# A hand-ordered step list for retention and a SoLU feed-forward block: zero products moved, steps re-ordered

## The chip, the cores and the metric

The kernel runs on one core of a Trainium2 chip. Its engines work from queues of their own and meet at semaphores: TensorE (PE: matrix products, with weight loads shown as PEld), VectorE (DVE), ScalarE (ACT), GpSimd (POOL) and SyncE (SP), which issues nearly all DMAs. The metric is the device time of one execution in microseconds; lower is better. The kernel before took 213.36 us as the median of three runs (212.89 to 214.8).

## The reference, cut to what matters

```python
# q, k, v: (8, 8, 576, 64) = batch, head, position, head_dim, float32
scores = q @ k.transpose(0, 1, 3, 2) / 8
D[h, i, j] = gamma[h] ** (i - j) if i >= j else 0      # gamma[h] = 1 - 2 ** (-5 - h)
x = (scores * D) @ v           # back to 4608 tokens x 512
h = x @ w_in                   # 512 -> 1024
e = exp(h - max(h));  sm = e / (sum(e) + 1e-9)
solu = h * sm
ln = (solu - mean(solu)) / sqrt(var(solu) + 1e-6) * g_ln
out = ln @ w_out               # 1024 -> 512, float32
```

First comes a retention (attention without softmax, with a decay by distance), then a feed-forward block with a softmax-weighted activation, a normalisation and a second product, for each of 4608 tokens.

## The kernel before, in words

**Tiles.** The tokens are cut into 18 tiles n = 0 to 17, each of 256 tokens in two halves i = 0, 1. Tiles 0 to 3 are the first 256 positions of four batch entries, 4 to 7 the next 256 of the same, 8 the last 64 of all four together; 9 to 17 repeat this for the other four entries. The retention is worked in chunks of 128 positions: products within a chunk, and a state that is carried from chunk to chunk.

**Steps.** The work on a tile is a set of small functions, each called a step. A word such as `mk:3.0.1` in the string ORDER (L744) calls step mk for tile 3, half 0, part 1; `@v`, `@s`, `@g` put it on VectorE, ScalarE or GpSimd. The words are run through once, each emits its instructions at that place in the queue of its engine, and nothing re-orders them later. So ORDER alone sets the order on every engine and on SyncE's DMA queue. A wait is added only where data or a buffer is needed, and it holds everything behind it on that engine.

For tile n the steps are:

- `lq`, `lk`, `lv` (L173): loads of 512 KB each from SyncE's queue, into 16 buffers that are used in turn; `wi`, `wo` load four chunks each of the two weights.
- `q`, `k`, `v` (L197, L152): casts to 16 bits, with the decay multiplied in where needed.
- `tp` (L239): 32 transposes of q and k on TensorE, copied out by two `qkT` steps (L150, L152); for some tiles a DMA transpose `dt` (L251) does both.
- `sc` (L265): 16 products q k within a chunk, for each half; `mk` (L276): four multiplications with the triangular mask, on VectorE.
- `kp` (L290): 32 products k v for the state; `t` (L305), `s32` (L314), `s16`: the state is added up, decayed and cast. `s32` is always on GpSimd.
- `xs` (L349): product with the carried state; `xv` (L364): 32 products of masked scores with v. Both write the same PSUM bank. `xT` copies the result out.
- `mm1` (L426): eight products with w_in (for tile 0's half 0 in four pieces of two, by chunk of w_in; `cwA` and `cwB` cast a chunk); `max` (L434), `exp` (L449), `solu` (L497), `nmu`, `sq` (L517), `w1`, `w2`, `pow`: softmax weight and normalisation.
- `lpj` (L584): 32 transposes, copied out by two `uTj` steps, or DMA transposes `du` (L591); `uc` subtracts the mean for the first tiles. `mm2` (L607): eight products with w_out, `osb` scales, `st` stores.
- `g32`, `ws`, `mean`, `mc`, `cw`: w_out is multiplied with g_ln and its mean taken off, early in the kernel. `gx` makes a decay table on ScalarE.

**Zero products.** `warm:k` (L720 to L729) issues k products of a tile of zeros, 128x128 by 128x512. They write the bank that the next step to take a bank will take, and that step overwrites them:

```python
junk = psum[:, int(BANKS[turns.get("bank", -1) + 1])]
zeros = s16s[:, 2 + 6 - 1].rearrange("p a e d -> p (a e d)")
for _ in range(k):
    nc.tensor.matmul(out=junk, lhsT=zeros[:, 0:P], rhs=zeros, start=True, stop=True)
```

There are 50 of them before, in eight groups: 21 before tp:0, 6 before sc:0.0, 4 before tp:1, 7 before tp:2, 2 before sc:2.1, 4 before kp:3, 4 before lpj:1 and 2 before lpj:2.

**Banks.** The string BANKS names, in the order in which steps ask for one, which of the eight PSUM banks a step gets.

The line numbers of the profile are those of the code below; in the changed kernel all lines behind ORDER stand one further down.

## Time and profile before

| | |
|---|---|
| median of 3 runs | 213.36 us (212.89 to 214.8) |
| the profiled execution, its time | 214.05 us |
| its span, first to last instruction | 212.3 us |
| TensorE busy, matmuls | 196.4 us (93%), 3154 |
| VectorE, ScalarE, GpSimd busy | 186.1, 171.0, 143.6 us |
| mean granted TensorE clock | 0.983 |
| products of `mm1` (L426) and `mm2` (L607) | 280 x 390 ns, 248 x 372 ns |
| zero products (L726) | 50, 379 ns each from start to end |
| bytes moved by DMA | 49.29 MB, mean 232 GB/s |

A profile page shows one execution. Busy shares are averages over the whole span; the stages have to be read apart, by slices or windows. Matmuls are pipelined: the time from the start to the end of one (379 ns) is longer than the time from one start to the next (216 ns at full clock), and the second is what a row of them costs. "Granted clock" is the share of full speed at which TensorE was allowed to run. A note such as `[0.54 <-ACT w_in L150]` behind an instruction says that its engine was idle for 0.54 us before it and that this ended when ScalarE's instruction of L150 was done; "issue" says that nothing which the profile shows was waited for.

### The profile page before, as it was taken

The page shows a single profiled execution, that of the slowest core. Times are in us where ns is not written, and L with a number is a line of the kernel's source. Part 1 is how long each engine was busy: PE and PEld are TensorE (multiplying, and loading weights), DVE is VectorE, ACT ScalarE, POOL GpSimd, SP SyncE. Part 2 cuts the span into 40 slices and gives each one's busy share as a digit, 9 for nine tenths or more (in the row PEclk, how much of TensorE's full clock was granted, in tenths as well). Part 3 has the DMA queues.
Part 4 walks back from the last instruction along what each step waited for, and adds up shares of the span by engine and source line. Part 5 has one row for each costly group of instructions (what it writes and reads, how often), then busy time and mean ns, then how long its engine had stood idle before and what let it go on. Part 6 is the DMA issues. An engine that isn't in the chain of part 4 may idle for free.

```text
span 212.3 us, 7613 instructions
## 1 busy us (share of the span) xinstructions
PE 196.4 (93%) x3154; PEld 103.2 (49%) x3154; DVE 186.1 (88%) x335; ACT 171.0 (81%) x288; POOL 143.6 (68%) x223
## 2 busy tenths in 40 slices
PE   4978979989998998999989999999999999999991
...
DVE  3499699999998999898979999999998999798960
...
PEclk9996799999999999999999999999999999999999
...
GB/s 162 290 383 310 281 296 367 295 259 262 138 217 183 213 209 216 320 293 223 249 327 164 285 236 316 279 197 246 264 203 217 238 99 179 171 148 115 85 198 150
DMA packets 90530, 49.29 MB, mean 232 GB/s; under 512 B 29440, under 2 KB 84992, under 8 KB 90496
## 3 DMA queue, kind: packets, MB, share of 16 engines
...
## 4 chain that ended last, share of the span: by engine, by line
PE 70%; DVE 14%; DMA 4%; SPq 4%; issue 3%; ACT 2%; POOL 1%; ACTq 0%; DVEq 0%; POOLq 0%
PE psum L426 25%; PE psum L607 24%; PE psum L265 5%; DVE nm L434 4%; PE psum L364 4%; DMA ld<-in_moe_w_in_dram 4%; PE psum L349 3%; PE psum L584 3%; SPq L173 3%; DVE u L497 2%; PE psum L290 2%; PE psum L239 1%; SPq L647 1%; PE psum L726 1%; DVE uc L553 1%
## 5 line engine op out<-in xcount | busy, mean ns | idle before, releaser
L426 PE MATMUL psum<-w_in,xT 128*128 128x512 f16 x280 | 68.5, 390 | 1.6 <-issue 0.7
L607 PE MATMUL psum<-w_out,uTj 128*128 128x512 f16 (+1 forms) x248 | 55.1, 372 | 0.0
L434 DVE TENSOR_REDUCE nm<-psum 128x1 f32<-128x1024 f32 x35 | 42.5, 1218 | 6.5 <-PE psum L426 6.1
L449 ACT ACTIVATE e<-psum,nm 128x1024 f32<-128x1024 f32 x35 | 39.0, 1114 | 11.0 <-DVE nm L434 9.2
L607 PEld LDWEIGHTS <-uTj 128*128 128x128 f16 x296 | 28.0, 98 | 31.0 <-issue 0.6
L497 DVE SCALAR_TENSOR_TENSOR u<-psum,e 128x1024 f16<-128x1024 f32 x35 | 42.0, 1216 | 0.4 <-ACT e L449 0.3
L517 ACT ACTIVATE sq<-u,nmu 128x1024 f16<-128x1024 f16 x35 | 40.3, 1150 | 1.2 <-DVE nmu L507 0.9
L426 PEld LDWEIGHTS <-xT 128*128 128x128 f16 x280 | 25.8, 100 | 31.3 <-issue 4.7
L540 POOL TENSOR_TENSOR rs<-w,mhalf 128x2 f32<-128x2 f32 x17 | 11.8, 696 | 38.0 <-DVE w L528 36.7
L197 POOL TENSOR_TENSOR v<-ld,small 128x512 f16<-128x512 f32 x29 | 30.4, 1057 | 4.6 <-DMA ld<-in_v_dram 3.5
L197 POOL TENSOR_TENSOR qk<-ld,small 128x512 f16<-128x512 f32 x24 | 25.0, 1050 | 1.1 <-DMA ld<-in_q_dram 0.6
L150 ACT COPY uTj<-psum 128x1024 f16<-128x1024 f16 (+1 forms) x18 | 17.3, 990 | 3.1 <-PE psum L584 3.1
L314 POOL TENSOR_TENSOR s32a<-t,small 128x256 f32<-128x256 f32 x16 | 10.6, 662 | 11.8 <-DVE t L152 6.9
L726 PE MATMUL psum<-s16s 128*128 128x512 f16 x50 | 14.2, 429 | 3.5 <-DVE s16s L853 3.1
L152 POOL CAST qk<-ld 128x512 f16<-128x512 f32 x25 | 15.4, 628 | 0.7 <-DMA ld<-in_k_dram 0.6
L150 ACT COPY qkT<-psum 128x1024 f16<-128x1024 f16 x12 | 12.0, 1018 | 4.7 <-PE psum L239 4.7
L265 PE MATMUL psum<-qkT 64*64 64x128 f16 x576 | 14.7, 223 | 0.2
L150 ACT CAST xT<-psum 128x512 f16<-128x512 f32 x24 | 13.3, 588 | 1.7 <-PE psum L349 1.0
L265 PEld LDWEIGHTS <-qkT 64*64 64x64 f16 x576 | 9.8, 107 | 7.5 <-issue 6.3
L364 PEld LDWEIGHTS <-v 64*64 64x64 f16 x576 | 9.3, 106 | 7.1 <-issue 6.8
L349 PE MATMUL psum<-qkT,s16s 128*128 128x128 f16 (+1 forms) x128 | 10.7, 216 | 1.6 <-POOL s16s L152 1.4
L314 POOL TENSOR_TENSOR s32b<-t,small 128x256 f32<-128x256 f32 x16 | 10.2, 640 | 2.0 <-DVE t L305 1.8
...
## 6 DMA issues: line engine op xcount, KB each, us to landing
...
```

What stands on the lines that cost most here:

```text
L150: nc.scalar.copy(out=out, in_=in_)
L197: vec(eng).tensor_tensor(out=to, in0=src, in1=tab[:, 8 * e : 8 * e + 8].unsqueeze(2).to_broadcast([P, H, D]), op=ALU.mult,)
L265: nc.tensor.matmul(out=s[o][cc, hp], lhsT=qkT_view(n, 1, c)[dd, e, hp], rhs=qkT_view(n, 0, c)[dd, :, hp], start=True, stop=True,)
L314: nc.gpsimd.tensor_tensor(out=s, in0=T["t", n, i], in1=gs.unsqueeze(2).to_broadcast([P, 4, D]), op=ALU.mult)
L349: nc.tensor.matmul(out=to, lhsT=state[:, hp].rearrange("p e d -> p (e d)"), rhs=rhs, start=first and hp == 0 and j == 0, stop=True, skip_g ...
L364: nc.tensor.matmul(out=x[c][oo, hp], lhsT=v16[cc, e, 2 * hp + o], rhs=T["ret", n, e, o][cc, hp], start=first[c] and e == 0 and hp == 0, st ...
L426: nc.tensor.matmul(out=h[:, a], lhsT=s[:, d], rhs=w_in16[:, d, a * 512 : (a + 1) * 512], start=r == 1, stop=r == 4,)
L434: nc.vector.tensor_reduce(out=nm, in_=T[key("h", n, i, j)], axis=AX.X if j is not None else AX.XY, op=ALU.max, negate=True)
L449: nc.scalar.activation(out=flat(e, j), in_=T[key("h", n, i, j)], func=ACT.Exp, bias=T["nm", n, i], accum_out=s)
L497: nc.vector.scalar_tensor_tensor(out=flat(u, j), in0=T[key("h", n, i, j)], scalar=1.0, in1=flat(T[key("e", n, i, j)], j), op0=ALU.mult, op ...
L517: nc.scalar.activation(out=t, in_=T[key("u", n, i, j)], func=ACT.Square, bias=T["nmu", n, i], accum_out=ss)
L607: nc.tensor.matmul(out=o, lhsT=T["uT", n, i][:, c], rhs=wt[:, c, a : a + w], start=c == 0, stop=c == NF - 1,)
```

## The change

Only the strings ORDER and BANKS differ. Every step of the computation is still there once, and no step's code is changed. There are 54 zero products instead of 50, in twelve groups: 17 before tp:0, 2 before sc:0.1, 3 before sc:0.0, 7 before tp:1, 2 before xv:0, 1 before sc:1.1, 10 before tp:2, 4 before xs:1.1, 2 before xv:1, 2 before kp:3, 1 before mm2:0.0 and 3 before xs:4.0. Some now stand ahead of `xs` and `xv`, where these are the first to write their bank. The other words are in a new order, most of all up to tile 9, and 67 steps run on another engine: among them 9 casts `k` go from GpSimd to ScalarE and 5 the other way, 4 casts `v` from VectorE to GpSimd, 4 `xT` from ScalarE to VectorE. From about tile 10 on the order is nearly the same. BANKS is a new assignment for the first two thirds.

The diff replaces all of ORDER; here are its beginning, two places in the middle and its end:

```diff
     ORDER = """
-        lk:0 gx lq:0 k:0.0@s k:0.1@g q:0.0@v lv:0 lq:1 q:0.1@v warm:21 tp:0 v:0.1@v v:0.0@v kp:0
-        q:1.1@v t:0.0@v s32:0.0 qkT:0.1@v qkT:0.0@s lk:1 k:1.0@v q:1.0@g warm:6 sc:0.0 t:0.1 wi:2
-        k:1.1@s sc:0.1 wi:0 wi:3 s32:0.1 mk:0.1.0 warm:4 tp:1 mk:0.0.0 mk:0.0.1 cwB:2@s s16:0.0@s
-        mk:0.1.1 xv:0 cwA:2@g wi:1 qkT:1.1@v cwA:0@v cwB:0@g xT:0.0@v cwB:3@g qkT:1.0@s sc:1.0
-        mk:1.0.1 xs:0.1 cwA:3@s mm1:0.0.3 lv:1 cwA:1@g xT:0.1@v s16:0.1@g cwB:1@s v:1.1@g mk:1.0.0
-        sc:1.1 mm1:0.0.0 lq:2 lk:2 q:2.1@g q:2.0@g mk:1.1.0 mm1:0.1 v:1.0@v mk:1.1.1 k:2.0@g
-        max:0.1 exp:0.1 mm1:0.0.2 mm1:0.0.1 max:0.0 k:2.1@v kp:1 t:1.0@s warm:7 tp:2 s32:1.0 lv:2
-        solu:0.1 v:2.1@v exp:0.0 s16:1.0@g qkT:2.1@s qkT:2.0@s t:1.1 v:2.0@g nmu:0.1 solu:0.0
-        xs:1.1 lq:4 xv:1 lv:3 lq:3 lk:3 xT:1.0@s nmu:0.0 warm:2 sc:2.1 sc:2.0 mk:2.1.0 xT:1.1@s
-        kp:2 q:4.1@g q:4.0@g s32:1.1 mk:2.0.0 t:2.0@s mk:2.1.1 mk:2.0.1 uc:0.1@s sq:0.1 mm1:1.1
-        s32:2.0 uc:0.0@v sq:0.0 max:1.1 xv:2 mm1:1.0 q:3.0@v xT:2.0@s exp:1.1 s16:2.0@g t:2.1
-        xs:2.1 max:1.0 xT:2.1@s solu:1.1 mm1:2.0 lpj:0 q:3.1@g max:2.0 wo:2 wo:0 v:3.0@g g32
-        k:3.1@g exp:1.0 mm1:2.1 solu:1.0 ws:4@s k:3.0@s wo:1 exp:2.0 w1:0@g v:3.1@g ws:0@g wo:3
-        ws:1@g ws:5@g ws:2@s w2:0 uTj:0.1@v uTj:0.0@v ws:3@s max:2.1 lk:4 w1:1@v nmu:1.1 nmu:1.0
-        ws:6@s warm:4 kp:3 ws:7@g t:3.0@s tp:3 solu:2.0 uc:1.0@v mm2:0.0 s32:3.0 qkT:3.0@s exp:2.1
-        s32:2.1 qkT:3.1@s lv:4 pow:0 t:3.1 k:4.1@s sq:1.0 mean k:4.0@g sc:3.1 sc:3.0 solu:2.1
-        nmu:2.0 mm2:0.1 v:4.1@v mc@s mk:3.1.0 mk:3.1.1 s16:3.0@g v:4.0@g lk:5 lk:6 mk:3.0.1
-        mk:3.0.0 sq:1.1 uc:1.1@s tp:4 s32:3.1 kp:4 lq:5 qkT:4.0@s cw:5@g xv:3 qkT:4.1@s osb:0.1@v
-        xs:3.1 t:4.0 warm:4 lpj:1 xT:3.1@s lq:6 cw:6@v sc:4.0 k:6.1@g nmu:2.1 xT:3.0@v s32:4.0
-        k:5.1@g lv:5 uTj:1.1@s s16:1.1@s cw:0@v uTj:1.0@s osb:0.0@s t:4.1 mk:4.0.0 uc:2.0@v mm1:3.0
-        w2:1 k:5.0@g q:5.1@g mm1:3.1 q:5.0@g pow:1 v:5.0@g s16:4.0@g max:3.0 uc:2.1@v s32:4.1 lk:7
-        sc:4.1 q:6.0@s q:6.1@s mk:4.0.1 v:5.1@g mm2:1.0 exp:3.0 max:3.1 st:0.1 lv:6 mk:4.1.0
-        mk:4.1.1 mm2:1.1 xv:4 w1:2@g xs:4.1 v:6.0@g solu:3.0 k:6.0@s v:6.1@g osb:1.0@s exp:3.1
-        solu:3.1 dt:5 kp:5 t:5.0 osb:1.1@s xs:4.0 tp:6 st:1.0 s16:2.1@g cw:1@v st:0.0 sq:2.0 kp:6
-        xT:4.1@s t:6.0 warm:2 lpj:2 s32:5.0 qkT:6.1@v t:5.1 xT:4.0@s qkT:6.0@s uTj:2.1@s cw:4@g
...
-        t:7.0 osb:3.1@s mm1:5.1 mk:7.0.0 sq:5.0 qkT:8.0@v nmu:4.0 sq:4.1 qkT:8.1@s sq:4.0 sc:7.1
-        mk:7.0.1 lv:9 s32:7.0 mm1:6.0 max:5.1 exp:5.1 s16:7.0@g mk:7.1.1 mk:7.1.0 max:6.0 lk:9
-        st:2.0 exp:6.0 st:2.1 s16:4.1@g q:9.1@g s16:3.1@g mm2:4.0 xs:7.0 s32:6.1 t:7.1 w2:4 pow:4
...
-        qkT:10.0@s qkT:10.1@v uTj:6.0@s mk:9.1.0 mk:9.1.1 w1:6@g sc:9.0 kp:10 mm1:8.0 max:7.1
-        mk:9.0.0 w2:6 t:10.0@s mk:9.0.1 lq:13 lk:12 s16:9.0@s q:11.0@g k:11.0@g s32:10.0 v:11.1@g
-        max:8.0 s32:9.1 xs:9.1 v:11.0@g exp:7.1 t:10.1 mm2:6.1 pow:6 st:5.0 s16:10.0@g w1:7@g
...
-        osb:15.1@v w2:17.0 w2:16 pow:16 w1:17.1 uT:17.1.0@s st:15.1 sq:17.1.1 sq:17.1.0 osb:16.1@v
-        pow:17.0 mm2:17.1.1 osb:17.0@s ssadd:17.1 w2:17.1 osb:16.0@v st:16.1 st:16.0 st:17.0
-        pow:17.1 osb:17.1.1@s mm2:17.1.0 st:17.1.1 osb:17.1.0@s st:17.1.0
+        lk:0 lq:0 k:0.0@v lv:0 lq:1 q:0.1@v q:0.0@v k:0.1@g warm:17 tp:0 v:0.1@v qkT:0.1@s
+        qkT:0.0@v v:0.0@g kp:0 gx warm:2 sc:0.1 warm:3 sc:0.0 lk:1 t:0.0@v mk:0.1.0 wi:0 q:1.1@g
+        q:1.0@g s32:0.0 mk:0.1.1 k:1.0@g mk:0.0.1 k:1.1@s s16:0.0@s warm:7 tp:1 xs:0.1 t:0.1
+        mk:0.0.0 cwA:0@v qkT:1.1@v cwB:0@s warm:2 xv:0 qkT:1.0@s wi:3 wi:2 warm:1 sc:1.1 s32:0.1
+        cwB:3@g xT:0.0@v mk:1.1.0 cwB:2@v sc:1.0 wi:1 cwA:3@s lv:1 cwA:2@g lq:2 xT:0.1@s mm1:0.0.3
+        mm1:0.0.0 cwA:1@v mk:1.1.1 mk:1.0.1 v:1.1@g mk:1.0.0 q:2.1@g lk:2 cwB:1@s k:2.0@g mm1:0.1
+        v:1.0@v max:0.1 exp:0.1 k:2.1@g lv:2 mm1:0.0.1 mm1:0.0.2 max:0.0 kp:1 t:1.0@s lq:3 s32:1.0
+        s16:1.0@g lk:3 exp:0.0 q:2.0@v solu:0.1 warm:10 tp:2 qkT:2.0@s warm:4 xs:1.1 nmu:0.1
+        qkT:2.1@s t:1.1 solu:0.0 v:2.1@v nmu:0.0 warm:2 xv:1 v:2.0@g sc:2.1 xT:1.1@s q:3.1@g kp:2
+        mk:2.1.1 sc:2.0 mk:2.1.0 w1:0@v lq:4 q:3.0@v mm1:1.1 sq:0.1 mk:2.0.1 mk:2.0.0 xT:1.0@s
+        t:2.0@s max:1.1 uc:0.0@v lv:3 uc:0.1@s s16:0.1@g s32:1.1 k:3.0@g k:3.1@g s32:2.0 s16:2.0@s
+        sq:0.0 mm1:1.0 t:2.1 w2:0 wo:0 xv:2 xs:2.1 max:1.0 xT:2.0@s mm1:2.0 exp:1.1 wo:3 xT:2.1@s
+        solu:1.1 exp:1.0 lpj:0 max:2.0 mm1:2.1 q:4.0@g g32 v:3.0@g v:3.1@g wo:1 uTj:0.1@v uTj:0.0@v
+        warm:2 kp:3 wo:2 ws:6@s solu:1.0 max:2.1 s32:2.1 tp:3 ws:0@g ws:7@g w1:1@g ws:1@g ws:3@s
+        exp:2.0 ws:4@s ws:2@s ws:5@g nmu:1.0 t:3.0@s solu:2.0 mean q:4.1@g lk:4 lq:5 uc:1.0@v
+        nmu:1.1 s32:3.0 lv:4 qkT:3.0@s warm:1 mm2:0.0 exp:2.1 mc@s qkT:3.1@s s16:3.0@g pow:0 t:3.1
+        k:4.0@g lk:5 k:4.1@s sc:3.1 solu:2.1 osb:0.0@s lv:6 sc:3.0 uc:1.1@s q:5.1@g tp:4 v:4.1@g
+        v:4.0@g mm2:0.1 cw:6@v mk:3.1.1 mk:3.0.1 mk:3.1.0 kp:4 k:5.1@g cw:5@g qkT:4.1@s mk:3.0.0
+        osb:0.1@v xv:3 v:6.1@g qkT:4.0@s t:4.0 sc:4.0 lpj:1 s32:4.0 xT:3.0@v s32:3.1 xs:3.1
+        mk:4.0.0 mk:4.0.1 sq:1.0 k:5.0@s lq:6 q:5.0@v xT:3.1@s mm1:3.0 lv:5 mm1:3.1 v:5.0@g v:6.0@g
+        max:3.0 sq:1.1 uTj:1.1@s lk:6 v:5.1@g k:6.1@g w1:2@g s16:4.0@g nmu:2.1 cw:0@v uTj:1.0@s
+        sc:4.1 t:4.1 max:3.1 q:6.0@s mk:4.1.0 nmu:2.0 mk:4.1.1 w2:1 exp:3.0 exp:3.1 k:6.0@s
+        warm:3 xs:4.0 q:6.1@s solu:3.0 solu:3.1 cw:1@v mm2:1.0 xv:4 xs:4.1 mm2:1.1 st:0.1 xT:4.0@s
+        xT:4.1@s kp:6 st:0.0 kp:5 uc:2.0@s uc:2.1@v t:6.0 s32:4.1 pow:1 cw:2@g tp:6 dt:5 osb:1.1@s
+        t:5.0 osb:1.0@s lpj:2 lk:7 lq:8 qkT:6.1@v lq:7 cw:7@v sc:5.0 s32:6.0 qkT:6.0@s t:6.1
+        mk:5.0.0 mm1:4.0 sq:2.0 uTj:2.0@s mm1:4.1 cw:3@v s32:5.0 cw:4@g q:7.0@g uTj:2.1@s sq:2.1
...
+        mk:7.0.1 osb:3.0@s st:2.1 w1:4@v qkT:8.1@v t:7.0 mk:7.0.0 mm1:5.1 sq:4.1 sc:7.1 qkT:8.0@s
+        mm1:6.0 s16:3.1@g v:8.1@g s32:7.0 q:9.0@g v:8.0@g q:9.1@g s32:5.1 w2:4 max:5.1 st:2.0
+        mk:7.1.0 k:10.0@s osb:3.1@s k:10.1@s s16:4.1@s mk:7.1.1 lk:9 exp:5.1 mm2:4.0 xs:7.0 lv:9
...
+        sc:9.0 kp:10 nmu:7.0 t:10.0@s sq:6.0 t:9.1 max:7.1 mk:9.0.0 mk:9.0.1 mm1:8.0 w2:6 s32:9.1
+        s16:9.0@g st:4.1 s32:10.0 max:8.0 mm2:6.1 t:10.1 s16:10.0@g exp:7.1 sq:7.0 solu:7.1
...
+        w2:17.0 w2:16 pow:16 w1:17.1 uT:17.1.0@v st:15.1 sq:17.1.0 osb:16.1@s sq:17.1.1 pow:17.0
+        mm2:17.1.1 osb:17.0@s ssadd:17.1 w2:17.1 osb:16.0@v st:16.1 st:16.0 st:17.0 pow:17.1
+        osb:17.1.1@s mm2:17.1.0 st:17.1.1 osb:17.1.0@s st:17.1.0
     """
...
     BANKS = "".join(
         """
-        765432765174630175237654736452316754230154673245345210765421076540156732473214065327640126
-        743025143761275463764521067531235076432016523767510643254016574237654103256743201765365721
-        034756201675436721045673210547623765401675473256107347652017654320176542365410756320174356
+        765476325176435201675432576432104567312310450176076354217645310725601327432765310247501675
+        435243150761276305674321045730176354210673201325764216574017654237654106523756401765362751
+        034726501675436721045673210547623765401765463257106347652017654320176542365410756320174356
         742340165746523765437653276
```

117 lines of the change are left out of this document (59 added, 58 removed).

## The prediction

> **What bounds the kernel now.** I read the page's 40 slices first. TensorE is at 9 tenths almost everywhere from slice 18 on and thinner before, and the granted clock has its one dip in slices 3 to 5:
>
> ```profile
> PE   4978979989998998999989999999999999999991
> DVE  3499699999998999898979999999998999798960
> PEclk9996799999999999999999999999999999999999
> ```
>
> The windows of 10 us (columns: stretch, length, busy us of PE, PEld, DVE, ACT, POOL, clock, DMA share, GB/s) give the stages.
>
> ```profile
> 20.00:30.00 10.00, 8.64 (x121) 3.82 (x117) 8.17 (x13) 4.16 (x7) 6.71 (x10) 0.78 1.11 284
> 40.00:50.00 10.00, 9.02 (x138) 4.38 (x138) 10.00 (x19) 9.31 (x16) 9.55 (x13) 1.00 1.04 271
> 70.00:80.00 10.00, 9.77 (x167) 5.57 (x167) 10.00 (x18) 8.69 (x15) 9.32 (x13) 1.00 1.16 224
> 140.00:150.00 10.00, 10.00 (x173) 5.46 (x170) 9.84 (x21) 9.94 (x16) 6.22 (x10) 1.00 0.95 243
> ```
>
> Up to 30 us nothing is full but the DMA; from 30 to 80 VectorE is, at 10.00 of 10 in three windows; from 120 to 200 TensorE has 10.00 in every window. TensorE's real products are the same in both kernels, so the time moves with what TensorE loses before about 112 us: idling, zero products (50, 0.216 us each at full clock) and half clock. I looked for these losses in TensorE's own waits and its timeline (start, us, what).
>
> ```profile
> 17.49 0.58 PE L349 MATMUL psum<-qkT,s16s 128*128 128x128 f16 x4
> 18.61 1.01 PE L426 MATMUL psum<-w_in,xT 128*128 128x512 f16 x2 [0.54 <-ACT w_in L150]
> 19.55 0.64 PE L265 MATMUL psum<-qkT 64*64 64x128 f16 x16
> 20.12 5.29 PE L426 MATMUL psum<-w_in,xT 128*128 128x512 f16 x14
> 25.34 0.45 PE L290 MATMUL psum<-v,qk 64*64 64x64 f16 x32
> 25.72 1.68 PE L726 MATMUL psum<-s16s 128*128 128x512 f16 x7
> 27.33 0.64 PE L239 MATMUL psum<-ident,qk 64*128 64x64 f16 x32
> 29.34 0.40 PE L349 MATMUL psum<-qkT,s16s 128*128 128x128 f16 x4 [1.36 <-POOL s16s L152]
> ```
>
> Fourteen mm1 products take 5.29 us: the clock is 0.5 from 17.75 to 24.39 us, each takes 0.427 instead of 0.216. The third loss has no partner:
>
> ```profile
> 66.90 0.45 PE L584 MATMUL psum<-ident,uc 64*128 64x64 f16 x19 [0.90 <-issue]
> 81.46 0.21 PE L364 MATMUL psum<-ret__1809,v 64*64 64x128 f16 x1 [0.73 <-issue]
> 110.64 0.82 PE L426 MATMUL psum<-w_in,xT 128*128 128x512 f16 x3 [0.74 <-issue]
> ```
>
> Counted from the start these are matmuls 991, 1247 and 1759, a multiple of 128 apart. The instruction queue (24 packets of 16 KB on the page) has a transfer starting 2.65 to 2.76 us before each (64.22, 78.81, 107.88). So TensorE stalls where it runs through 128 matmuls faster than the next packet comes; from one such boundary to the next it needed 4.29, 5.16 and 6.10 us.
>
> **The change, step by step.** Only the order, engines and banks move; 54 zero products replace 50. Durations are rows of before.
>
> *Start to xv:0.* 17 zero products instead of 21 before tp:0: its casts are done at 8.51, the zeros hold it to 9.81; 4 x 0.216 fewer give 8.95. The two qkT:0 copies were ScalarE 10.49 to 11.50 and VectorE 11.70 to 12.38, behind t:0.0 and a cast; now ScalarE runs one at once (9.6 to 10.6, gx after it; its table load has no wait left ahead of it) and VectorE the other. sc:0.1 then ends at about 11.2. The masks, which ended at 16.50 behind k:1.0 (1.26), end near 14.1. But tp:1 still waits for k:1.0, now on GpSimd at 14.06 (before 13.97), and xs:0.1 stands ahead of xv:0, so xv:0 ends near 16.0 instead of 16.96.
>
> *First mm1.* The four w_in chunks land as before (13.77 to 18.77), so the last casts end at 19.4 and 19.9. Then 11 products at 0.216 end mm1 at 21.8; before, 10 at 0.427 ran from 20.19 to 24.46. max:0.1 starts near 22.0 instead of 24.58, behind v:1.0 (0.69); the wait of cwA:1 on VectorE until 18.77 holds three masks of tile 1 behind it, which nobody needs before xv:1. This holds if the clock stays up: before, between 14.2 and 17.6 us, TensorE had tp:1, xv:0 and sc:1.0, some 1.4 us of work (0.57, 0.46, 0.36 by their spacing); after, xs:0.1, three zero products and sc:1.1 (0.33, 0.65, 0.36) join them, 2.7 us. A stretch from 27.9 with a 1.36 us gap and some 2.3 us of work in 3.4 kept 1.00, so I take full clock. If not, mm1 ends at 24.2, and kp:1 and *ten* zeros stand ahead of tp:2: at half clock that is up to 4.3 us, and tp:2 comes at 27.1.
>
> The Trainium skill ("TensorE: Matmul & The Clock Gate", Part 1) says that one idle window of about 3.4 us halves the clock and a busy one restores it, by windows that run free of the kernel; the changes at 17.75 and 24.39, 6.64 us apart, fit two of them. Its Part 4 says transposes don't count as busy in the same way, which speaks against this change: without tp:1 only 2.1 us are left, under the 2.3 that held, and the sum would be that of the second rival. No row here tells the two apart.
>
> *Tiles 1 and 2.* lk:2 lands at 24.29; both casts on GpSimd (2 x 0.61) make tp:2 25.6 instead of 27.33, and the ten zeros (2.2 us from 22.4) lie beside that wait. s32:1.0 and s16:1.0 (0.61, 1.2) follow, so xs:1.1 starts at 27.3 instead of 29.34 and xv:1 ends at 28.6 instead of 30.30. **Lead at 30 us: 1.7 to 2.0.** Loads of tiles 2 to 4 came 2.3 to 4.6 us before their use, so they allow it.
>
> *30 to 86 us.* VectorE's steps ahead of a milestone, summed with their rows, shrink: 2.5 us fewer before mm1:3.0, 2.1 before max:4.0, 1.8 before solu:5.0 (casts to GpSimd and ScalarE). Worked along the chains by the same rows, mm1:3.0 starts at 51.6 (54.05), tp:6 at 62.0 (64.14), mm1:5.1 at 83.5 (86.7). Two places eat some of it: GpSimd has 4.8 us more ahead of xv:6, and w2:2 makes VectorE wait 1.1 us for sq:2.1, with mk:5.1.0 and max:4.1 queued behind. SyncE's queue gains too: dt:5, with the loads lq:8 and lq:7 behind it, waited for q:5.0 until 57.2; that cast now ends at 52.9. I take a **lead of 2.9 at 86 us**, the packet at matmul 991 (0.3 of its 0.9 left) included.
>
> *86 to 112 us.* What VectorE was spared comes back: 3.3 us more between solu:5.0 and max:8.0. It was busy 24.60 of the 28 us from 84 to 112, so with the lead it would have no idle time at all: cost 0.3 (bounds 0 and 2). And the packets: between boundaries TensorE's work was 2.78, 4.07 and 5.41 us in the three stretches that stalled; after it is 3.71, 4.43 and 4.27, the third because one mm1:8.0 product instead of five lies ahead of the boundary. If that packet needs its 6.10 again, TensorE stalls 1.8 instead of 0.74: cost 1.1 (bounds -0.7 and 1.9).
>
> *After 112.* The order is nearly the same. VectorE has 1.5 to 2.4 us more in all, against 7.0 idle between 100 and 200; banks and the end (last copy, last store) cost nothing that I can find: bounds +-0.4.
>
> **Sum:** -2.9 + 0.3 + 1.1 = -1.5. The profiled execution took 214.05 (span 212.3 and 1.75 around it), so 212.5 there; against the median 213.36, which is 0.7 lower, **211.8**.
>
> **Rivals.**
> 1. *The packets come in time* (the fetch at 112 is as quick as 4.29 at 66): 213.4 - 2.9 + 0.3 with the old 0.74 is 210.8, without any stall 210.0; I take 210.3. For it, most boundaries pass without a stall; against it, DMA share 1.22 at 110 to 120.
> 2. *The clock falls again* at the first mm1, or a late load eats the lead: the ten zeros run at half clock, tp:2 27.1, xv:1 29.9, lead 0.4, the packet cost remains: about 213.6, no change. It is weighed above; the skill's Part 4 gives this time.
> 3. *Slower: packets.* If each packet after 60 us takes as long as the slowest seen (6.10), the five short stretches (3.71, 4.43, 4.27, 5.60, 5.49) stall 7.0 us in all, where before lost 2.37: 4.6 more, less the lead of 2.6: 215.4, up to 217 where two more are late. From a packet time of about 5.7 it outweighs the lead. Against it: stretches of 5.3 and 5.9 us late in the trace passed without a stall.
>
> That the order does not do what it says can only be rival 2: the zeros are issued, but may not hold the clock.
>
> **How the numbers follow.** Forecast 0.45 (210.8 to 212.8), rival 1 0.20 (209.3 to 210.8), rival 2 0.20 (212.8 to 214.5), rival 3 0.15 (214.5 to 217). Ranges meet where the bounds do. 8 in 10: 209.7 to 214.9 leaves out some 5 in 100 below and 13 above. One per cent, about what a measurement can tell, lies at 211.2 and 215.5: faster is rival 1 and four tenths of the forecast's share, 0.38; slower two thirds of rival 3, 0.10, and 0.02 for a stall I did not see; same 0.50.
>
> **What would show it.** tp:0 at 8.9; clock 1.00 through 17 to 25 us; max:0.1 near 22; xv:1 ended by 28.6 and mm1:5.1 started near 83.5; an "issue" stall inside mm1:8.0 near 108 to 110, longer than 0.74; then TensorE at 10.00 per 10 us. The prediction is wrong if the clock dips at 17 us, if VectorE or GpSimd holds mm1:4 to 6, or if stalls by "issue" sum to over 5 us.

## The result and the profile after

| | before | after |
|---|---|---|
| median, 20 executions each | 213.04 us (210.93 to 215.79) | 213.83 us (212.49 to 218.04) |
| ratio after / before | | 1.0062, 95% interval 1.0033 to 1.0091 |
| profiled execution, span | 214.05, 212.3 us | 213.82, 212.1 us |
| mean granted clock of the profiled execution | 0.983 | 0.999 |
| TensorE busy | 196.4 us | 194.4 us |

The forecast was 211.8 us, 0.7% below the median of before; measured is 0.6% above. That is inside the range given (209.7 to 214.9), but the sign is wrong. Ratios and intervals in this document leave out executions over 1.5% above the fastest of their kernel (eight of e3's twelve, four of e4's); medians and ranges are over all.

The page of the changed kernel, its 40 slices for TensorE, VectorE and the granted clock:

```profile
PE   4897996899979999999889999999999999999991
DVE  4589998999888999999998999979998999898940
PEclk9999999999999999999999999999999999999999
```

The dip (the 6 and the 7 of before, 16 to 27 us) is gone; slices 20 and 21 (101 to 111 us) have an 8 each. The windows of the changed kernel, with the same columns as before:

```profile
20.00:30.00 10.00, 9.11 (x192) 4.88 (x191) 9.96 (x17) 5.63 (x9) 7.65 (x10) 1.00 1.10 285
40.00:50.00 10.00, 9.29 (x206) 5.05 (x208) 10.00 (x19) 9.93 (x16) 9.79 (x13) 1.00 1.11 283
70.00:80.00 10.00, 9.58 (x201) 5.91 (x200) 10.00 (x20) 9.02 (x15) 9.56 (x16) 1.00 1.02 206
100.00:110.00 10.00, 8.74 (x225) 5.13 (x223) 9.39 (x19) 9.02 (x16) 6.51 (x12) 1.00 1.18 273
140.00:150.00 10.00, 9.09 (x164) 4.95 (x163) 9.22 (x19) 9.87 (x17) 6.32 (x10) 1.00 0.87 248
```

From 20 to 30 us there are 192 products instead of 121, at clock 1.00. But from 100 to 110 TensorE idles 1.26 us (9.90 busy before), and from 140 to 150, where it had been full (10.00), 0.91. TensorE's timeline names these losses:

```profile
103.31 0.64 PE L239 MATMUL psum<-ident,qk 64*128 64x64 f16 x32 [0.58 <-DVE uTj L152]
...
106.77 0.38 PE L426 MATMUL psum<-w_in,xT 128*128 128x512 f16 x1
107.82 1.67 PE L426 MATMUL psum<-w_in,xT 128*128 128x512 f16 x7 [0.68 <-issue]
...
143.53 0.42 PE L265 MATMUL psum<-qkT 64*64 64x128 f16 x16 [0.84 <-DVE u L497]
```

The first is tp:10, waiting for a bank that uTj:6.1 empties late. The second is matmul 1759, an instruction packet. The third is sc:13.1, waiting for a bank that solu:10.1 empties late.

**Where the lead went.** One execution of the kernel before (e6 below) had no clock dip: 211.46 us. The table gives the start of some steps in each profile less the start in that one, in us (negative is earlier).

| step (start without the dip) | before, profiled | after | after, k:15.0 on GpSimd | that, without four zeros |
|---|---|---|---|---|
| max:0.1 (21.88) | +2.71 | +0.38 | +0.30 | +0.44 |
| mm1:3.0 (51.83) | +2.22 | -0.47 | -0.56 | -0.49 |
| mm1:6.0 (86.59) | +2.24 | -0.59 | -0.67 | -0.62 |
| tp:10 (103.02) | +2.24 | +0.29 | +0.20 | +0.23 |
| mm1:8.1 (113.83) | +2.60 | +0.87 | +0.35 | +0.02 |
| mm1:9.1 (123.89) | +2.59 | +1.06 | +0.54 | +0.20 |
| mm1:11.1 (141.94) | +2.59 | +2.17 | +0.54 | +0.20 |
| last store (206.13) | +2.59 | +2.39 | +0.75 | +0.41 |

Against the profiled execution of before, the changed one is 2.83 us ahead at mm1:6.0 (2.24 + 0.59), 1.53 at mm1:9.1, 0.42 at mm1:11.1 and 0.20 at the end. Against the kernel before without its dip it is 0.6 us ahead at mm1:6.0 and 2.4 behind at the end.

### The profile page after: what moved, and what is told of

It is laid out like the page before. It is cut to its first block, busy times and chain, and to the rows that moved or that the text cites. A ratio compares the mean times of both kernels' runs of the same rounds, so it can differ in the third digit from the quotient of the medians.

```text
span 212.1 us, 7622 instructions
## 1 busy us (share of the span) xinstructions
PE 194.4 (92%) x3158; PEld 103.0 (49%) x3158; DVE 187.8 (89%) x339; ACT 170.9 (81%) x288; POOL 142.9 (67%) x219
## 4 chain that ended last, share of the span: by engine, by line
PE 40%; DVE 5%; ACT 3%; issue 2%; ACTq 0%; DVEq 0%
PE psum L607 16%; PE psum L426 14%; PE psum L265 2%; DVE u L497 2%; PE psum L364 2%; PE psum L349 2%; DVE nm L434 1%; PE psum L239 1%; ACT uTj L150 1%; PE psum L416 1%; PE psum L584 1%; PE psum L290 1%; ACT sq L517 1%; DVE xT L386 1%; PE psum L564 0%
## 5 line engine op out<-in xcount | busy, mean ns | idle before, releaser
L426 PE MATMUL psum<-w_in,xT 128*128 128x512 f16 x280 | 65.8, 379 | 3.7 <-ACT xT L150 1.3
L426 PEld LDWEIGHTS <-xT 128*128 128x128 f16 x280 | 25.6, 98 | 31.9 <-issue 2.8
L197 POOL TENSOR_TENSOR v<-ld,small 128x512 f16<-128x512 f32 x32 | 34.4, 1085 | 5.7 <-DMA ld<-in_v_dram 5.0
L197 POOL TENSOR_TENSOR qk<-ld,small 128x512 f16<-128x512 f32 x22 | 23.4, 1067 | 1.2 <-DMA ld<-in_q_dram 0.9
L726 PE MATMUL psum<-s16s 128*128 128x512 f16 x54 | 15.6, 423 | 3.1 <-DVE s16s L854 3.1
L150 ACT CAST xT<-psum 128x512 f16<-128x512 f32 x21 | 12.1, 585 | 4.8 <-PE psum L364 3.0
L152 POOL CAST qk<-ld 128x512 f16<-128x512 f32 x23 | 14.9, 659 | 1.1 <-DMA ld<-in_k_dram 1.1
L150 ACT COPY uTj<-psum 128x1024 f16<-128x1024 f16 (+1 forms) x16 | 15.2, 985 | 0.5 <-PE psum L584 0.5
L150 ACT CAST qk<-ld 128x512 f16<-128x512 f32 x20 | 12.2, 621 | 1.8 <-DMA ld<-in_k_dram 1.8
```

The lines of the kernel that those rows point to most:

```text
L150: nc.scalar.copy(out=out, in_=in_)
L197: vec(eng).tensor_tensor(out=to, in0=src, in1=tab[:, 8 * e : 8 * e + 8].unsqueeze(2).to_broadcast([P, H, D]), op=ALU.mult,)
L426: nc.tensor.matmul(out=h[:, a], lhsT=s[:, d], rhs=w_in16[:, d, a * 512 : (a + 1) * 512], start=r == 1, stop=r == 4,)
```

## The experiments

Times in us; the fourth column is the median of those executions whose mean granted clock was 0.994 or more, and how many of all these are. The kernel before ran beside every group: of its 139 executions 39 had such a clock (median 212.1), 49 had 0.987 to 0.994 (212.8), 51 less (214.4).

| kernel | median (range) | ratio to before, 95% | at clock 0.994 or more |
|---|---|---|---|
| changed kernel | 213.83 (212.49 to 218.04) | 1.0062 (1.0033 to 1.0091) | 213.7, 18 of 20 |
| e12, changed again | 214.02 (212.77 to 218.31) | 1.0064 (1.0028 to 1.0099) | 213.8, 8 of 12 |
| e1, before again | 213.92 (212.7 to 215.83) | 1.0064 (1.0023 to 1.0105) | none of 12 |
| e2, k:15.0 on GpSimd | 213.39 (212.2 to 215.59) | 1.0053 (1.0014 to 1.0091) | 213.1, 9 of 12 |
| e3, 11 zeros less | 216.88 (211.93 to 219.06) | 1.0006 (0.9955 to 1.0057) | 212.3, 2 of 12 |
| e4, before and 7 zeros | 214.2 (211.6 to 216.71) | 1.0024 (0.9975 to 1.0073) | 212.8, 5 of 12 |
| e7, VectorE relieved | 214.79 (213.99 to 217.67) | 1.0094 (1.0058 to 1.0131) | 214.3, 6 of 12 |
| e8, tail's engines as before | 214.09 (213.83 to 216.67) | 1.0055 (1.002 to 1.009) | 214.0, 10 of 12 |
| e9, before, 7 zeros moved | 213.75 (212.58 to 215.42) | 1.0029 (0.9996 to 1.0062) | 212.6, 1 of 12 |
| e10, k:15.0 and four zeros less | 212.07 (211.63 to 213.62) | 0.9961 (0.9926 to 0.9996) | 211.9, 10 of 12 |
| e11, four zeros less | 213.0 (212.24 to 214.19) | 0.9995 (0.9961 to 1.0029) | 212.8, 8 of 12 |
| e13, four opening zeros less | 212.24 (211.77 to 213.45) | 0.9972 (0.9941 to 1.0002) | 212.2, 11 of 12 |
| e14, four opening zeros more | 213.16 (211.99 to 214.56) | 1.0017 (0.9988 to 1.0046) | 213.2, 12 of 12 |
| e15, e10 again | 212.54 (211.81 to 214.23) | 0.9991 (0.9958 to 1.0024) | 212.3, 9 of 12 |
| e16, e10 and w1:5, w1:6 | 212.35 (211.86 to 213.51) | 0.9967 (0.9937 to 0.9996) | 212.2, 8 of 12 |

Groups on one chip in one go: e1 to e4; e5 to e8; e9 to e11; e12 to e15; e16. Only inside a group do kernels compare side by side; the groups ran on four chips in all.

### The clock dip: is it there in every execution?

*e1, e5 and e6 are the kernel before, unchanged.*

> The kernel before, unchanged, timed against itself. Theory A (the profiled execution of before was one with a clock dip that most executions do not have): the profile, or the executions with a mean granted clock of 0.995 or more, show 210.9 to 212.3 us and TensorE at full clock through 17 to 25 us; executions at about 0.983 show 213.5 to 215. Theory B (the dip is always there, the scatter of before comes from elsewhere): clock near 0.983 in all, and no relation of clock and time.

> The kernel before once more, one look for its profile. Theory A (the dip of the clock is the whole of the changed kernel's lead): where this execution has a mean clock of 0.995 or more, it takes 211.5 to 212.5 us, max:0.1 starts near 22.5 instead of 24.58 and mm1:6.0 near 87 instead of 88.8. Theory B (the lead is the order's): mm1:6.0 stays near 88.5 though the clock is full. With a dip again it tells nothing new.

> As e5: a second chance to see the kernel before in an execution without the dip, with the same numbers expected by the two theories.

Measured: e1 213.92, its twelve executions all at a clock of 0.971 to 0.991; e5 212.55 at 0.989; e6 211.46 at 0.994. The page of e6, the kernel before in an execution without the dip:

```profile
PE   4977879899997998999999999999999999999991
PEclk9999999999999999999999999999999999999997
```

The clock stays at 9 or more in every slice but the last, and the end is 2.59 us earlier than in the profiled execution of before. Nearly all of it is there from max:0.1 on (table above, first column). So the dip costs 2.2 to 2.6 us and belongs to an execution, not to the kernel. It comes in two sizes: in the profiles of before and e1 the clock is 0.50 for 6.8 us (17.57 to 24.39 in before; the prediction read 17.75), in e5 for 3.4 us (18.58 to 21.99). Half clock for 6.8 us takes 0.016 off the mean of 212 us, for 3.4 us 0.008, which fits the three groups of clocks above (an estimate). The same code, run against itself in e1, gives a ratio of 1.0064, where the change gave 1.0062, because all of e1's twelve executions have a dip. So a difference of 0.6% says nothing here by itself.

The Trainium skill ("TensorE: Matmul & The Clock Gate", Part 1, "What's actually happening") says that the window which decides on the clock runs free of the kernel, and that the same kernel therefore shows different numbers of slow matmuls. The executions of before, with mean clocks from 0.971 to 1.0 for identical code, agree.

### Do zero products hold the clock?

*e3: the changed kernel without its zeros ahead of xv:0, xs:1.1, xv:1 and xs:4.0.*

```diff
-  cwB:0@s warm:2 xv:0 ... qkT:2.0@s warm:4 xs:1.1 ... nmu:0.0 warm:2 xv:1 ... k:6.0@s warm:3 xs:4.0
+  cwB:0@s xv:0 ... qkT:2.0@s xs:1.1 ... nmu:0.0 xv:1 ... k:6.0@s xs:4.0
```

> The changed kernel without the eleven zero products that stand ahead of xv:0, xs:1.1, xv:1 and xs:4.0. Theory A (they hold the clock up at 17 to 25 us): the clock falls to 0.5 there in the profile or in some of the executions, mean clock near 0.98, and the time is 0.5 to 2 us longer in those. Theory B (the clock is held by the other changes, or the dip depends on where the clock's windows fall): clock 0.995 and more, and the time within 0.5 us of the changed kernel, or up to 0.6 less since TensorE has 11 x 0.216 us less to do.

Measured: ten of twelve executions have a clock of 0.971 to 0.992 and a median of 217.2; the two at 0.995 and 0.996 took 211.93 and 212.66. In the changed kernel 18 of 20 keep the clock, in e12 8 of 12, and in e2, beside e3, 9 of 12. So without these zeros the clock falls far more often. Where it falls is not shown, for e3's profile is of the execution at 0.995. So it is open, too, why those ten took 5 us longer, more than the 2.2 of before; ten zeros ahead of tp:2 at half speed, as in the prediction's second rival, are one candidate.

*e4: the kernel before with seven zeros more; e9: the same, with seven opening zeros less, so that later products keep their number.*

```diff
-  q:0.1@v warm:21 tp:0 ... mk:0.1.1 xv:0 ... qkT:1.0@s sc:1.0 ... cwA:3@s mm1:0.0.3
+  q:0.1@v warm:21 tp:0 ... mk:0.1.1 warm:2 xv:0 ... qkT:1.0@s warm:3 sc:1.0 ... cwA:3@s warm:2 mm1:0.0.3     (e4)
+  q:0.1@v warm:14 tp:0 ... mk:0.1.1 warm:2 xv:0 ... qkT:1.0@s warm:3 sc:1.0 ... cwA:3@s warm:2 mm1:0.0.3     (e9)
```

> The kernel before with seven more zero products: 2 ahead of xv:0, 3 ahead of sc:1.0 and 2 ahead of mm1:0.0.3, nothing else changed. Theory A (the dip costs before 2 us where it comes, and more zeros prevent it): mean clock 0.995 and more in all executions, median 211.5 to 212.3, that is 0.5 to 1.5 faster than before. Theory B (the dip hides behind the loads, it costs nothing at the end): the same time as before within 0.4 us.

> The kernel before, with seven of its 21 opening zero products taken away (the others still end near 8.3 us, before the casts that tp:0 waits for, 8.5) and seven put where TensorE was thin: 2 ahead of xv:0, 3 ahead of sc:1.0, 2 ahead of mm1:0.0.3. The number of products ahead of every later instruction packet is the same as before, so no boundary moves. Theory (the change's gain is the clock dip at 17 to 25 us alone, its loss is the rest of the new order): without the dip this order takes about 212.0; if the zeros hold the clock in nearly all runs, the median is 211.8 to 212.4, 0.6 to 1.0 below the kernel before and 1.2 to 1.8 below the changed one. If seven zeros hold it in half of the runs only, as in the run that added them without taking any away, the median is 213 and the runs at a clock of 0.995 or more lie at 211.3 to 212.5. Rival (the full clock itself is not the gain, the runs of before near 212 are quick for another reason): runs with the clock at 0.995 or more take 213 or longer.

Measured: e4 keeps the clock in 5 of 12 executions (the kernel before beside it in 9 of 35), e9 in 1 of 12 (the others 0.987 to 0.992). My theories for both fell: the medians are 214.2 and 213.75, not 212. So in the old order seven zeros at these places do not hold the clock. The windows of e9's profile (columns as above) suggest why:

```profile
24.00:26.00 2.00, 1.72 (x37) 0.83 (x34) 2.00 (x4) 1.78 (x4) 1.32 (x3) 1.00 1.04 283
26.00:28.00 2.00, 0.28 (x4) 0.23 (x4) 2.00 (x6) 2.00 (x4) 1.81 (x4) 1.00 1.14 294
28.00:30.00 2.00, 2.00 (x69) 1.37 (x70) 1.17 (x4) 1.68 (x3) 2.00 (x3) 0.75 1.16 290
30.00:32.00 2.00, 2.00 (x48) 1.11 (x41) 2.00 (x4) 1.19 (x2) 1.94 (x4) 0.50 1.16 318
```

The place at 17 us is held, but TensorE is busy for only 0.28 of the 2 us from 26 to 28, waiting for s16, and the clock falls right behind. In this execution the dip is at 29 us, not at 17. The changed order has zeros there too (four ahead of xs:1.1, two ahead of xv:1), and in none of its profiles does the clock fall there.

A thin stretch does not always bring a dip. From 34 to 36 us TensorE is busy for only 0.40 to 0.71 of the 2 us in all twelve profiles of the changed order and its variants; the clock falls behind it in two (e11, e16) and stays up in ten. And a stall further back can be followed by a dip as well: behind 1.88 us without work at matmul 1759 in e8's profile the clock is 0.50 from 109.24 to 112.65 us, behind 2.58 us in e4's from 110.28 to 113.69. So a low mean clock does not say where it was lost. Whether transposes count for the clock, which the prediction left open, none of these runs tells.

### k:15.0 on ScalarE

*e2: one cast of the changed kernel back on GpSimd.*

```diff
-  k:15.0@s v:13.0@g uTj:9.0@s uTj:9.1@s
+  k:15.0@g v:13.0@g uTj:9.0@s uTj:9.1@s
```

> The changed kernel with one cast put back: k:15.0 on GpSimd instead of ScalarE. In the profile of the changed kernel ScalarE waits 1.5 us in front of it for a load that lands at 135.9, with uTj:9.0, uTj:9.1, sq:9.0 and exp:10.1 queued behind, and TensorE's lead over before falls from 1.53 to 0.42 us. Theory A (the lead is lost at this wait): 1.0 us faster than the changed kernel, about 212.8, sc:13.1 without the 0.84 us gap ahead of it. Theory B (VectorE is short of time there anyway, and would hold the banks as late): 0.0 to 0.3 faster.

*e10: the same, and one zero ahead of mm2:0.0 and three ahead of xs:4.0 left out; e11: these four zeros out, k:15.0 as in the change.*

```diff
-  qkT:3.0@s warm:1 mm2:0.0 ... k:6.0@s warm:3 xs:4.0 ... k:15.0@s
+  qkT:3.0@s mm2:0.0 ... k:6.0@s xs:4.0 ... k:15.0@g     (e10)
+  qkT:3.0@s mm2:0.0 ... k:6.0@s xs:4.0 ... k:15.0@s     (e11)
```

> The changed kernel with k:15.0 back on GpSimd, and without one zero product ahead of mm2:0.0 and three ahead of xs:4.0, so that from matmul 991 on the instruction packets end where they do before: five mm1:8.0 products ahead of matmul 1759, not one. If the place of the boundary costs time: with 0.9 us more work ahead of it the stall at 1759 (0.68 in the changed kernel, 0.27 with k:15.0 alone) goes, but stalls of up to 0.9 can come at 991 and 1247, where the kernel before has them; at full clock 212.4 to 213.0, against 213.1 for k:15.0 alone. If the packets cost nothing in all: 213.1 as with k:15.0 alone, or 212.5 if the three zeros ahead of xs:4.0 were on the path. If the rest of the loss is in VectorE's steps between 97 and 107 us, this stays about 1 us above the undisturbed kernel before (212.0).

> The changed kernel without the same four zero products, k:15.0 on ScalarE as in the change. If the two losses add, this lies 1.0 to 1.4 above the kernel with k:15.0 on GpSimd in the same session, and 0 to 0.7 below the changed kernel's 213.6 at full clock: 213.0 to 213.6, with the gap at sc:13.1 (0.84) as it was. If a later start of the tail hides k:15.0's wait, the two differ by less than 0.4.

Measured: e2 took 213.39, 0.44 less than the changed kernel (0.6 at full clock, at another time), between its two theories. e11 less e10, which differ in k:15.0 alone and ran side by side, is 0.93 us (213.0 and 212.07), 0.84 at full clock; 1.0 or more had been expected. ScalarE's timeline in the changed kernel shows the wait:

```profile
133.87 0.59 ACT L150 CAST xT<-psum 128x512 f16<-128x512 f32 x1
136.00 0.62 ACT L150 CAST qk<-ld 128x512 f16<-128x512 f32 x1 [1.54 <-DMA ld<-in_k_dram]
136.52 1.92 ACT L150 COPY uTj<-psum 128x1024 f16<-128x1024 f16 x2
138.33 1.16 ACT L517 ACTIVATE sq<-u,nmu 128x1024 f16<-128x1024 f16 x1
...
139.48 1.11 ACT L449 ACTIVATE e<-psum,nm 128x1024 f32<-128x1024 f32 x1
```

The cast of k:15.0 stands ahead of two uTj copies, sq and exp:10.1, and its load lk:15 lands only at 135.9. ScalarE idles 1.54 us, and the four steps behind it, whose inputs are there, wait with it. VectorE then waits for that exp:

```profile
139.29 0.14 DVE L507 TENSOR_SCALAR nmu<-su 128x1 f32<-128x1 f32 x1
140.71 1.23 DVE L497 SCALAR_TENSOR_TENSOR u<-psum,e 128x1024 f16<-128x1024 f32 x1 [1.27 <-ACT e L449]
```

So solu:10.1 is late, its bank is free late, and sc:13.1 stands still for 0.84 us. In e10, with the cast on GpSimd, ScalarE goes straight on:

```profile
133.01 0.59 ACT L150 CAST xT<-psum 128x512 f16<-128x512 f32 x1
133.72 1.93 ACT L150 COPY uTj<-psum 128x1024 f16<-128x1024 f16 x2
135.54 1.16 ACT L517 ACTIVATE sq<-u,nmu 128x1024 f16<-128x1024 f16 x1
...
136.89 1.11 ACT L449 ACTIVATE e<-psum,nm 128x1024 f32<-128x1024 f32 x1
```

The exp comes 2.6 us earlier where the whole kernel is 0.9 us earlier (mm1:9.1), and TensorE has no wait between 140 and 146 us.

How much this costs depends on when lk:15 lands: ScalarE waits 1.54 us for it here, 1.09 in e12 and 0.99 in e11, and sc:13.1 then stands still for 0.84, 0.47 and 0.37. Nor does GpSimd make the cast free. It waits for the load as well, 1.7 to 2.2 us in e2, e10, e13 and e15, and there nothing on TensorE's path is behind it; but in e14's profile (below) the load lands at 137.5, GpSimd waits 3.73 us, and TensorE stands 0.81 us for the cast of v behind k:15.0.

### Four zeros, 40 us before the place where they cost

e2, with those four zeros, takes 213.1 at full clock, e10 211.9, but they ran at different times. And two causes remained: the zeros' own time, or the shift of every later product by four places against the instruction packets. Four kernels side by side tell these apart. e12 is the changed kernel and e15 is e10. The other two have k:15.0 on GpSimd:

```diff
-  q:0.0@v ... warm:17 tp:0 ... warm:1 mm2:0.0 ... warm:3 xs:4.0
+  q:0.0@v ... warm:13 tp:0 ... warm:1 mm2:0.0 ... warm:3 xs:4.0     (e13: the later zeros stay, products numbered as in e10)
+  q:0.0@v ... warm:21 tp:0 ... mm2:0.0 ... xs:4.0                   (e14: the later zeros are out, products numbered as after)
```

> The changed kernel once more, beside the three others on one chip. Its median was 213.83. If the four zeros and k:15.0 explain its loss, it lies 1.5 to 2.0 above the kernel without them (212.07), its stall at matmul 1759 is 0.5 to 1.0 and the gap ahead of sc:13.1 0.8. If that kernel was quick because of its session, the difference is under 0.8.

> k:15.0 on GpSimd, the zeros ahead of mm2:0.0 and xs:4.0 left in, and four of the 17 opening zeros taken away instead (tp:0's casts, done near 8.5, still come after the last of them): the packets end where they do in the kernel without the four later zeros. Theory (the place of the packet boundary costs the time): 212.0 to 212.4 and no stall at 1759. Rival (the three zeros ahead of xs:4.0 themselves held the matmuls behind them): 212.9 to 213.2, as with k:15.0 alone.

> The kernel with k:15.0 on GpSimd and without the four later zeros, but 21 opening zeros instead of 17: the packet boundaries are those of the changed kernel again. Theory (the boundary): a stall of 0.3 to 0.9 at matmul 1759 and 212.6 to 213.1. Rival (the later zeros' own time): 212.0 to 212.2, the opening zeros being beside w_in's loads, which mm1:0.1 waits for until 19 us.

> k:15.0 on GpSimd, the four later zeros taken out, as in the run of 212.07: the control for the two kernels with other opening zeros. 211.8 to 212.3 if that result holds on another occasion; near 213 if it was the session.

Measured: e12 214.02, e14 213.16, e15 212.54, e13 212.24. e12 lies 1.5 above e15, so the gain was not the session's. e13 keeps the later zeros and is as quick as e15, so their own time does not show: the number of the products matters, not where the zeros stand. e14 points the same way: at full clock 213.2 against 212.2 and 212.3 (e13, e15). This half is weaker: e14's executions (211.99 to 214.56) overlap e15's (211.81 to 214.23), and its profile, of its slowest execution, is already 0.35 us behind e15's at tp:10 and loses 0.81 at the late load named above. TensorE's timeline around mm1:8.0, eight products, in e14:

```profile
107.05 0.38 PE L426 MATMUL psum<-w_in,xT 128*128 128x512 f16 x1
108.19 1.67 PE L426 MATMUL psum<-w_in,xT 128*128 128x512 f16 x7 [0.76 <-issue]
```

in e12:

```profile
106.67 0.38 PE L426 MATMUL psum<-w_in,xT 128*128 128x512 f16 x1
108.86 1.67 PE L426 MATMUL psum<-w_in,xT 128*128 128x512 f16 x7 [1.81 <-issue]
```

and in e13:

```profile
106.96 1.89 PE L426 MATMUL psum<-w_in,xT 128*128 128x512 f16 x8
```

With one mm1:8.0 product ahead of matmul 1759 TensorE stalls in all six profiles, with five and the same wait for tp:10 in none of four: four products of 0.216 us give the packet 0.86 us more. Taken from one boundary to the next and without the stall itself, the stretch ahead of 1759 is 5.13 to 5.14 us in the five profiles with one product ahead and the same wait for tp:10 (stalls 0.27, 0.68, 0.76, 1.81, 1.88), and 5.78 to 5.83 in e10, e11, e13 and e15 (none). In the order of before, with five products ahead but no such wait, it is 5.36, and TensorE stalls there too (0.74 in before; 0.16, 0.40, 0.38 and 1.27 in e1, e5, e6 and e9). The same kernel stalled 0.68 in one execution and 1.81 in another, so what a packet needs, 5.4 to 7.1 us here, is not a constant.

The instruction queue in the traces shows what varies. The transfer itself takes 0.97 to 1.19 us, and where TensorE stalls, matmul 1759 comes 2.4 to 2.8 us after its start. But it starts anywhere from 2.9 (e2) to 4.4 us (e16) behind the boundary before: 3.24 in the changed kernel's profile, 4.17 in e12's. In e10, e11, e13 and e15 it started early, 3.0 to 3.2 us behind, and came just in time; by these numbers a start at 4.2 would stall them too, by about 1 us (an estimate). What makes the start late stays open; no run changed the traffic of the other queues at that place alone.

The Trainium skill ("Runtime: NRT & Kernel Launch", "Instruction fetch mechanics") says that TensorE's instructions come in blocks of 16 KiB, 256 instructions, fetched by the engine's own queue, and that crossing a block costs little, mostly hidden. The size agrees: 24 packets of 16 KB, a boundary every 128 matmuls with their 128 weight loads. The cost agrees at most boundaries, but not at this one, where TensorE stalls for up to 1.88 us in the changed order. Side by side, four products more or fewer ahead of it made 0.6 to 1.0 us of the median (e14 against e15 and e13).

### VectorE between 95 and 107 us, and the tail

The lead of 0.6 us at mm1:6.0 turns into 0.3 behind at tp:10. Three kernels look for the cause.

*e7: the changed kernel with k:15.0, w1:5, w1:6, q:11.0, v:11.0 on GpSimd, osb:4.1 and xT:7.1 on ScalarE. e8: 27 steps from v:11.0 on, k:15.0 among them, on the engines that they had before.*

```diff
-  w1:5@v  osb:4.1@v  xT:7.1@v  w1:6@v  q:11.0@v  v:11.0@v  k:15.0@s
+  w1:5@g  osb:4.1@s  xT:7.1@s  w1:6@g  q:11.0@g  v:11.0@g  k:15.0@g     (e7)
-  v:11.0@v osb:6.1@s k:12.1@g s16:11.0@g ... uT:17.1.1@s uT:17.1.0@v osb:16.1@s
+  v:11.0@g osb:6.1@v k:12.1@s s16:11.0@s ... uT:17.1.1@v uT:17.1.0@s osb:16.1@v     (e8, 27 words)
```

> The changed kernel with seven steps taken off the engines that got them: k:15.0, w1:5, w1:6, q:11.0 and v:11.0 to GpSimd, osb:4.1 and xT:7.1 to ScalarE, as before. Theory A (between 86 and 112 us VectorE is what runs out, since w1 there takes 0.8 and 1.04 us beside a GpSimd step instead of 0.2): TensorE's lead over the profiled execution of before is still 2.6 us at tp:10 and 2.2 at mm1:9.0 (1.95 and 1.71 in the changed kernel), and the time is 0.5 to 0.9 us shorter than with k:15.0 alone, about 212.4. Theory B (GpSimd or the loads hold those steps as late): within 0.3 us of k:15.0 alone.

> The changed kernel with all 27 changes of engine behind max:8.0 put back as before, the order kept. Theory A (the lead goes at single places, of which k:15.0 is the one behind 112 us): as with k:15.0 alone within 0.4 us, about 213.1. Theory B (the engine loads of the second half as a whole cost the changed kernel its lead): 0.5 to 1.2 us faster than k:15.0 alone.

Measured: 214.79 and 214.09. Neither is better than e2, which has k:15.0 alone (213.39); e7 is worse by 1.2 at full clock (on another chip, where the kernel before at full clock was slower by 0.3). In e7's profile mm1:6.1 waits 1.05 us for the xT copy now on ScalarE, and the stall at 1759 is 1.72. The theory that relieving VectorE as a whole gives the time back fell. So did the idea that the other engine changes of the tail cost 0.5 or more: with them put back the ratio to before is 1.0055, with k:15.0 alone 1.0053.

The two small steps remain. VectorE's and, below it, GpSimd's timeline of the changed kernel:

```profile
101.62 1.04 DVE L491 TENSOR_TENSOR w<-s 128x2 f32<-128x2 f32 x1
102.58 0.68 DVE L152 COPY uTj<-psum 128x1024 f16<-128x1024 f16 x1
```

```profile
101.60 1.05 POOL L197 TENSOR_TENSOR qk<-ld,small 128x512 f16<-128x512 f32 x1
```

w1:6 works on two numbers per partition, takes 1.04 us on VectorE and ends when the GpSimd step beside it ends; on GpSimd it takes 0.19. Behind it stands uTj:6.1, which frees tp:10's bank.

*e16: e10 with w1:5 and w1:6 on GpSimd.*

```diff
-  w1:5@v ... w1:6@v
+  w1:5@g ... w1:6@g
```

> The kernel with k:15.0 on GpSimd and without the four later zeros, and now w1:5 and w1:6 also on GpSimd, as before the change. On VectorE they took 0.8 and 1.03 us, each ending with the GpSimd step beside it, where GpSimd itself needs 0.19; w1:6 holds uTj:6.1, whose bank tp:10 waits for (gap 0.58). Theory (w1:6 on VectorE takes the lead of 0.6 at 97 us): the gap ahead of tp:10 goes, tp:10 starts 0.5 to 0.6 earlier (102.7 instead of 103.26), all that follows too, and the median is 211.6 to 212.1, against 212.07 and 212.54 in two sessions. Rival (VectorE's other work fills the place, or the next packet boundary takes it back): the gap shrinks, but from max:8.0 on the lead is within 0.2 of what it was, 212.1 to 212.5.

Measured: 212.35, ratio 0.9967 (0.9937 to 0.9996), no better than e10. TensorE's timeline of e16:

```profile
102.90 0.64 PE L239 MATMUL psum<-ident,qk 64*128 64x64 f16 x32
...
106.28 1.25 PE L426 MATMUL psum<-w_in,xT 128*128 128x512 f16 x5
109.35 0.81 PE L426 MATMUL psum<-w_in,xT 128*128 128x512 f16 x3 [1.81 <-issue]
```

The wait ahead of tp:10 is gone, as the theory had it, and tp:10 is early (102.90; 0.12 ahead of before without its dip instead of 0.23 behind, though this execution had a clock dip ahead of it). But then matmul 1759 stalls 1.81 us: without the wait the stretch ahead of it is 5.24 us, not 5.8. The rival was right in its result, and the profile points to why: the wait of 0.58 at tp:10 had been time that the packet needed. Here the packet's transfer started 4.4 us behind the boundary; had it started 3.15 behind, as in e10, the stall would have been about 0.5, as long as the wait that was taken away (an estimate). It is one profile of one execution; e7, which has no wait at tp:10 either, stalled 1.72.

Two of these versions, e10 and e16, have medians of 212.07 and 212.35 and intervals that just leave out 1; e10 again had 0.9991. They beat the changed kernel (by 1.5 us side by side, e12 against e15) and are 0 to 0.4% below the kernel before, which fits that they keep the clock in most executions. Without a dip, at 211.9 to 212.3, they are not quicker than the kernel before without one, 212.1.

## Why the prediction was wrong, step by step

*Start to xv:0: right.* tp:0 started at 8.77 (8.95 forecast), the masks of tile 0 were done at 14.62 (14.1), xv:0 ended at 16.32 (16.0).

*First mm1, tiles 1 and 2: right.* TensorE's timeline of the changed kernel:

```profile
19.76 2.53 PE L426 MATMUL psum<-w_in,xT 128*128 128x512 f16 x11 [1.33 <-DVE w_in L152]
22.39 0.45 PE L290 MATMUL psum<-v,qk 64*64 64x64 f16 x32
22.77 2.33 PE L726 MATMUL psum<-s16s 128*128 128x512 f16 x10
25.47 0.76 PE L239 MATMUL psum<-ident,qk 64*128 64x64 f16 x32 [0.37 <-DVE qk L197]
27.42 0.40 PE L349 MATMUL psum<-qkT,s16s 128*128 128x128 f16 x4 [0.21 <-POOL s16s L152]
```

Eleven products at full clock, max:0.1 at 22.26 (22.0), ten zeros beside the wait for k:2, tp:2 at 25.47 (25.6), xs:1.1 at 27.42 (27.3). xv:1 ended at 28.82 (28.6): a lead of 1.5, a little under the 1.7 to 2.0 forecast.

*30 to 86 us: right but for one place.* mm1:3.0 came at 51.36 (51.6), mm1:5.1 at 83.84 (83.5). tp:6 came at 63.01, not 62.0: at 60.29 TensorE waits 1.26 us for GpSimd's s16, which the working did not have, but the lead comes back behind it. The lead over the profiled execution was 2.83 at mm1:6.0; 2.9 was forecast.

*86 to 112 us: places right, sizes wrong, in opposite directions.* VectorE's part was put at 0.3 and the lead lost 0.88 by tp:10; w1:6, held up by GpSimd for 0.8, was not in the working. The packet step named the place, one mm1:8.0 product ahead of the boundary. It forecast a stall of 1.8 instead of 0.74, a cost of 1.1; in the profiled pair the stall was 0.68 instead of 0.74 and cost nothing. In other executions of this order it was 0.27 to 1.88, so 1.8 does come, but the working took one packet's time, 6.10, for all of them. The stretch is 5.14 us long, not the 4.27 worked out, mostly since the wait of 0.58 at tp:10 lies in it. Together 1.4 of lost lead were forecast and 1.3 are there (2.83 to 1.53 at mm1:9.1): that the sums agree is luck.

*After 112: the step that failed first.* "Banks and the end ... cost nothing that I can find: bounds +-0.4". From mm1:9.1 to the end the lead fell from 1.53 to 0.20, 1.3 us, and k:15.0 is 0.9 of it by the medians of e10 and e11. I had summed VectorE's work in the tail and not read what stands in ScalarE's queue behind a cast that waits for a load. The row was there: the profile of before has k:15.0 start on GpSimd at 135.60, 0.15 us after its load had landed, and it holds up nothing on ScalarE, which goes on to uTj:9.0. Bounds of 0.4 either way had no row behind them.

*The sum against the median: the step that failed next.* I took 1.5 from the profiled execution and moved the result by the 0.7 between it and the median. But what the change took away in that profile, 2.2 us of half clock, is there in full in about a third of the executions of before (clock under 0.987: 51 of 139, 214.4), in part in another third, and not in 39 (212.1). The changed kernel has no dip in 18 of 20 executions, and its median, 213.83, is by chance its profiled time. So the gain in the median was about 0.9 us (213.04 against 212.1 without a dip), not 2.2. With both steps put right the sum is 211.8 + 1.3 + 0.7 = 213.8; this is book-keeping after the fact, no second forecast.

*The rivals.* The clock did not fall again in the changed kernel, so the second did not occur, although its time of 213.6 is near the one measured; e3 shows that this order can lose the clock, not where. The third, packets as the whole of a slowdown, is half right: the boundary at 1759 stalled up to 1.88, but those at 991 and 1247 did not stall at all in the changed kernel. The measured time fell in the stated range only because the range allowed for these two. One chance was summed wrongly: 211.2 cuts off a fifth of the forecast's 210.8 to 212.8, not four tenths, so "faster" was 0.29 by the prediction's own ranges, not 0.38.

In short, at full clock the changed order is 1.6 us slower than the one before (213.7 against 212.1). Taking out k:15.0's place on ScalarE gives back 0.8 to 0.9, and four products fewer ahead of the boundary 0.6 to 1.0, side by side. Its better clock buys back about 0.9 in the median.
